# Attention score tiles of 128 queries of one head instead of 64 queries of two heads

## The chip, the cores and the metric

The kernel runs on one core of a Trainium2 chip. The metric is device time in microseconds (us) of one execution. Three runs of the kernel before took 1049.56, 1049.65 and 1050.9 us; their median is 1049.65.

## The reference

Attention with a block-causal mask feeds two dense layers. Everything is float32.

```python
B, H, S, D = 4, 8, 576, 64
scores = (1 / np.sqrt(D)) * np.matmul(q, k.transpose(0, 1, 3, 2))
mask = block_i >= block_j          # blocks of 64 positions
scores = np.where(mask, scores, -1e9)
attn = np.exp(scores - scores.max(-1, keepdims=True))
attn = attn / (attn.sum(-1, keepdims=True) + 1e-09)
x = np.matmul(attn, v)             # then to 2304 tokens x 512
h = x @ w_in                       # 512 -> 2048
x = (h - np.tanh(h)) @ w_out       # 2048 -> 512
xn = x / rms(x) * rms_g
g = xn @ w_gate; val = xn @ w_val  # 512 -> 1536 each
out = (silu(g) * val) @ w_out2     # 1536 -> 512
```

A query in block n (64 queries) sees the keys of blocks 0 to n.

## The kernel before

**Stages.** Tokens are taken in six groups of 384. Group b (0 to 3) holds queries 0 to 383 of batch b; groups 4 and 5 hold queries 384 to 575 of two batches each. A `Unit` is one batch's part of a group: part 0 (queries 0 to 383) or part 1 (384 to 575). It is worked in four head pairs p. So there are 16 head pairs of part 0 and 16 of part 1. Group 0's attention runs alone at the start, until about 49 us. After it the loop over s = 0 to 95 does the first dense layer, 16 column blocks per group (L913 to L915, L706 to L708, L716 in group 0), and `aslot` puts steps of the next groups' attention between its matmuls; attention ends near 549 us. The second dense layer with its weights follows, from about 616 us to the end.

**Light and heavy.** Units of groups 0 and 1 are light: one float32 matmul per product (two instructions in the trace). The others are heavy: a value is split into a high and a low part in fp32r, and a product is three matmuls (high by high, high by low, low by high).

**Scores (L473 to L513).** A score tile holds 64 queries of both heads of the pair: its stationary operand is a block-diagonal q (`qbd`, or `qlight` for light units; 128 rows, of which head 0 fills rows 0 to 63 of its columns and head 1 rows 64 to 127), and the moving operand is k of both heads, one above the other on the 128 rows. Tile n has exactly the keys that its queries see, 64(n+1) of them: 64, 128, 192, 256, 320, 384 in part 0, and 448, 512, 576 in part 1 (576 as two spans of 288 in two PSUM banks). So no masking is needed. VectorE takes the scaled minimum out of PSUM (L495), ScalarE the exponential with its sum (L497), GpSimd zeroes the unused half of the last block (L500), and after three tiles the reciprocal of the sums is taken (L505, L506) and the tiles are scaled, by GpSimd if light (L511), by ScalarE if heavy (L513).

**Turning (L515 to L532).** TensorE transposes each tile in 128x128 blocks (L526); ScalarE and VectorE write them to `pp`, split in high and low if heavy (L102, L107). **Value products.** `av` (L534) does one head per step; the light form `av_light` (L571, matmul in L579) uses v of one head, 64 columns, as the stationary operand and writes partitions 0 to 63 (head 0) or 64 to 127 (head 1) of one bank, six instructions a step.

**Order.** TensorE's order is the program's. `plan` (L370) writes the list of steps: three score tiles make a period, and a period's tiles are turned two periods later, with the value products (`a`) of a head pair behind its last scores. `upto` (L401) releases the steps by a cost (keys + 150 for a score tile or a turning, 400 for a value step) over the 61 slots of a group. The other engines' order is found by a planner with a timeline. PSUM has 8 banks `t` in the first stage, and 5 after it, shared by scores, turnings, value products and the first layer's `h`. `zero_q` (L211) zeroes the unused halves of the six q tiles at the start.

Of the kernel before, what the change touches and what calls it, by code (L numbers as in the profile page):

```python
# [53 lines left out]
AVLEAD = 3  # L54


class Unit:


    def __init__(self, b, part):  # L60
        self.b = b
        first, last = (0, 6) if part == 0 else (6, 9)
        self.q0, self.q1 = 64 * first, 64 * last
        self.nq = self.q1 - self.q0
        self.tiles = [(64 * (i + 1), i // 2 + 1) for i in range(first, last)]
        self.halves = [range(a, a + 3) for a in range(0, len(self.tiles), 3)]
        self.nk = self.q1
        self.nb = -(-self.nk // 128)
        self.group = b if part == 0 else B + b // 2
        self.light = self.group < 2  # L70
        self.off = 0 if part == 0 else 192 * (b % 2)

    def offset(self, ti):
        return 128 * sum(self.tiles[t][1] for t in range(ti // 3 * 3, ti))

    def blocks(self, pp, x, ti):

        c, nb = 64 * ti, self.tiles[ti][1]
        if self.q0:
            return pp[:, 0:nb * 768].rearrange("p (j h x c) -> p j h x c", j=nb, h=2, x=2)[:, :, :, x, c:c + 64]  # L80
        a, c = c // 256 * 256, c % 256
        r = pp[:, a:a + 3584].rearrange("p (h x r) -> p h x r", h=2, x=2)[:, :, x, 0:nb * 256]
        return r.rearrange("p h (j c) -> p j h c", j=nb)[:, :, :, c:c + 64]
# [10 lines left out]
def build(ctx, tc, q, k, v, w_in, w_out, w_gate, w_val, w_out2, rms_g, ident_in, out):  # L94
# [84 lines left out]
    qbd = [[at.tile([128, 6, 2, 64], F32R, name=f"q{x}{n}", bufs=1) for x in "hl"] for n in range(2)]  # L179
    lq = tc.tile_pool(name="lq", bufs=1, side="right")  # L180
    lqp = lq.__enter__()
    qlight = [lqp.tile([128, 6, 2, 64], F32, name=f"qf{n}") for n in range(2)]
# [28 lines left out]
    def zero_q():  # L211
        def none(t, hh):
            return t[64 * hh:64 * hh + 64, :, 1 - hh, :]
        for hh in range(2):
            for t in qlight:
                POOL.memset(none(t, hh), 0.0)
            for t in sum(qbd, []):
                POOL.tensor_copy(out=none(t, hh), in_=none(qlight[0], hh))

    def diag(t, hh, nq):  # L220
        return t[64 * hh:64 * hh + 64, 0:nq // 64, hh, :]

    def part(t, hh, nq):
        return t[64 * hh:64 * hh + 64, 0:nq].rearrange("p (i c) -> p i c", c=64)
# [4 lines left out]
    def reorder(name, src, eng):  # L229

        t = at.tile([128, S], F32, name=name, tag=name, bufs=1)
# [18 lines left out]
    def tr_prep(u, p, d):  # L250
# [12 lines left out]
        def q1():  # L263
            ps = tr(0)
            for hh in range(2):
                rnd(DVE if u.light and (hh == 0 or u.group or p) else ACT, diag(d["q"][0], hh, TG), part(ps, hh, TG))
            if not u.light:
                for hh in range(2):
                    lo(DVE, diag(d["q"][1], hh, TG), part(ps, hh, TG), diag(d["q"][0], hh, TG))
# [6 lines left out]
    def load_kq(src, b, p, name, r0, r1):  # L276
        t = at.tile([128, S], F32, name=name, tag=name)
# [7 lines left out]
    def kq_loads(u, p):  # L285
        d = {}
        if by_rows(u):
            for name, src in (("kr", k), ("qr", q)):
                d[name] = at.tile([128, S], F32, name=name, tag=name)
# [43 lines left out]
    def unit_prep(u, p, d):  # L333
# [14 lines left out]
        def q1():  # L348
            qt = at.tile([128, S], F32, name="qt", tag="qt", bufs=1)
            DVE.transpose(qt[:, 0:nq], qr[:, 0:nq])  # L350
            for hh in range(2):
                rnd(ACT, diag(d["q"][0], hh, nq), part(qt, hh, nq))
            for hh in range(2):
                lo(DVE, diag(d["q"][1], hh, nq), part(qt, hh, nq), diag(d["q"][0], hh, nq))

        return [(None, k1), (None, k2), (("s", 1, -1), q1), None, *values_prep(u, d)]

    class Attn:
# [11 lines left out]
        def plan(self, units):  # L370
# [5 lines left out]
            for i, (u, p) in enumerate(self.pairs):  # L376
                for half in u.halves:
                    period.setdefault(m, ([], [], []))[0].extend(("s", i, t) for t in half)
                    period.setdefault(m + 2, ([], [], []))[1].extend(("t", i, t) for t in half)
                    m += 1  # L380
                period.setdefault(m + 2, ([], [], []))[2].extend(("a", i, hh) for hh in range(2))
            for n in sorted(period):
                sc, tr, av = period[n]
                self.seq += sc[0:2] + av + tr[0:1] + sc[2:3] + tr[1:]
            self.cost = [0]
            for m, (kind, n, t) in enumerate(self.seq):
# [3 lines left out]
                self.cost.append(self.cost[-1] + (u.tiles[t][0] + 150 if kind in "st" else 400))  # L390
# [33 lines left out]
        def prep(self, cur):  # L424
            self.value(-1)
            if not self.preps and self.nextprep < len(self.pairs) and self.nextprep <= cur + 1:
# [4 lines left out]
                self.loads[i]["q"] = qlight[i % 2:i % 2 + 1] if u.light else qbd[i % 2]  # L431
# [41 lines left out]
        def scores(self, i, u, ti, d):  # L473
            keys, nb = u.tiles[ti]
            q, kh = d["q"], d["kh"]
            terms = [(q[0], kh)] if u.light else [(q[0], kh), (q[0], d["kl"]), (q[1], kh)]
            spans = [(0, keys)] if keys <= 512 else [(0, keys // 2), (keys // 2, keys)]
            sts = []
            for a, z in spans:
                s = env["t"].tile([128, 512], F32, name="t", tag="t")  # L480
                for n, (x, y) in enumerate(terms):
                    PE.matmul(s[:, 0:z - a], lhsT=x[:, ti].rearrange("p h c -> p (h c)"), rhs=y[:, a:z],  # L482
                              start=(n == 0), stop=(n == len(terms) - 1))
                sts.append((s, a, z))
            if ti == 0:
                d["st"] = at.tile([128, 24], F32, name="stat", tag="stat", bufs=3)
            if ti % 3 == 0:
                d["pt", ti // 3] = at.tile([128, 1664], F32, name="pt", tag="pt", bufs=3)
            st = d["st"]
            off = u.offset(ti)  # L490
            pt = d["pt", ti // 3][:, off:off + nb * 128]
# [807 lines left out]
```

## Time and profile before

| what | value |
|---|---|
| median of three runs | 1049.65 us |
| profiled execution | 1050.38 us |
| its span, first to last instruction | 1048.6 us |
| TensorE matmul busy | 1024.9 us |
| VectorE, ScalarE, GpSimd busy | 780.7, 664.6, 351.4 us |
| granted TensorE clock, mean | 1.000 of full |

The span is what the trace covers; 1.8 us of the profiled execution lie around it. In the timeline and in the groups PE is TensorE's matmul side and PEld its weight loading, which runs beside it. Matmuls are pipelined: the length of one is from its start to the modelled end of its results, so what one costs in a stream is read from the distance between starts.

### The profile page before, as it was taken

To read this page: it belongs to the slowest core of one execution; us is meant where nothing else is said; L and a number is where in the kernel's file an instruction comes from. 1 tells how busy PE (TensorE), PEld (TensorE's weight loads), DVE (VectorE), ACT (ScalarE), POOL (GpSimd) and SP (SyncE) were. 2 spreads that over 40 slices of the span, in tenths; PEclk is the share of its full clock that TensorE was granted. 3 is DMA by queue.
4 is the path that set the end of the run, shared out by engine and by line. 5 is a ranking of instruction groups with operands and counts; after the bars stand their busy time and mean duration, and the time that the engine had idled before them with its cause. 6 is when DMAs were issued, how large, how long until landed. Compare 5 with 4: busy or idle time off the path is not lost.

```text
span 1048.6 us, 18052 instructions
## 1 busy us (share of the span) xinstructions
PE 1024.9 (98%) x6014; PEld 934.2 (89%) x6014; DVE 780.7 (74%) x1557; ACT 664.6 (63%) x1533; POOL 351.4 (34%) x467
## 2 busy tenths in 40 slices
PE   8899999999999999999999999999999999999998
PEld 5666668998889889998999989998999999999998
DVE  5988857776787776788667889877876668666775
ACT  6977768788888877788858666443742147422253
POOL 5621111123343233334432443448211281111710
PEclk9999999999999999999999999999999999999999
DMA  9998899979777599768759979799698757876654
GB/s 217 273 291 286 269 295 268 295 207 281 208 229 208 138 256 288 216 205 289 263 167 341 358 262 347 266 352 348 228 328 300 270 197 263 309 268 247 257 220 144
DMA packets 190958, 274.03 MB, mean 261 GB/s; under 512 B 109456, under 2 KB 151184, under 8 KB 184464
## 3 DMA queue, kind: packets, MB, share of 16 engines
q1 hardware_dynamic: 190864, 272.87, 79.4%
q8 instruction: 48, 0.79, 0.3%
q14 instruction: 46, 0.38, 0.1%
HBM read 209.39 MB, written 63.44 MB: 260 GB/s over the span
## 4 chain that ended last, share of the span: by engine, by line
PE 70%; DVE 12%; DMA 7%; ACT 7%; issue 4%; POOL 0%; DVEq 0%; SPq 0%; ACTq 0%; POOLq 0%
PE t L482 5%; PE t L913 5%; PE t L915 4%; PE t L914 4%; PE acc L706 4%; PE acc L708 4%; PE acc L707 4%; PE gv L1014 4%; PE gv L1016 4%; PE gv L1015 4%; PE t L526 3%; PE ga L708 2%; PE ga L706 2%; PE ga L707 2%; PE t L550 2%
## 5 line engine op out<-in xcount | busy, mean ns | idle before, releaser
L913 PE MATMUL t<-xh,w 128*128 128x384 f32 x384 | 137.2, 357 | 0.9 <-DVE pp L107 0.8
L915 PE MATMUL t<-xh,w 128*128 128x384 f32 x384 | 129.6, 338 | 0.0
L914 PE MATMUL t<-xl,w 128*128 128x384 f32 x384 | 129.3, 337 | 0.0
L1014 PE MATMUL gv<-xh,ws 128*128 128x384 f32 x308 | 103.4, 336 | 2.3 <-DMA ws<-w2d 2.3
L1016 PE MATMUL gv<-xh,ws 128*128 128x384 f32 x308 | 103.4, 336 | 0.0
L1015 PE MATMUL gv<-xl,ws 128*128 128x384 f32 x308 | 103.4, 336 | 0.0
L706 PE MATMUL acc<-w,gh 128*128 128x512 f32 x240 | 98.7, 411 | 1.5 <-ACT gh L102 1.2
L497 ACT ACTIVATE pt<-pt,stat 128x64 f32<-128x64 f32 (+2 forms) x144 | 80.4, 559 | 23.5 <-DVE pt L495 22.7
L708 PE MATMUL acc<-w,gl 128*128 128x512 f32 x240 | 94.9, 396 | 0.3 <-DVE gl L107 0.3
L707 PE MATMUL acc<-w,gh 128*128 128x512 f32 x240 | 94.4, 393 | 0.0
L1068 ACT ACTIVATE gt<-c 128x384 f32<-128x384 f32 x29 | 15.2, 524 | 117.2 <-DVE c L1067 117.2
L1071 POOL TENSOR_TENSOR g<-va,vb 128x384 f32<-128x384 f32 x29 | 31.1, 1073 | 147.6 <-ACT va L1070 136.6
L495 DVE TENSOR_SCALAR_CACHE_REDUCE pt<-t 128x64 f32<-128x64 f32 (+2 forms) x144 | 64.0, 450 | 20.4 <-PE t L482 19.4
L913 PEld LDWEIGHTS t<-xh,w 128*128 128x128 f32 x384 | 72.3, 188 | 5.1 <-DVE pp L107 1.2
L914 PEld LDWEIGHTS t<-xl,w 128*128 128x128 f32 x384 | 72.4, 189 | 2.3
L915 PEld LDWEIGHTS t<-xh,w 128*128 128x128 f32 x384 | 72.1, 188 | 0.0
L102 ACT ACTIVATE pp<-t 128x512 fp32r<-128x512 f32 (+6 forms) x152 | 63.0, 436 | 11.1 <-PE t L526 10.7
L107 DVE TENSOR_TENSOR pp<-t,pp 128x512 fp32r<-128x512 f32 (+3 forms) x112 | 55.2, 509 | 17.2 <-ACT pp L102 16.7
L526 PE MATMUL t<-ident,pt 128*128 128x128 f32 x400 | 65.7, 273 | 2.1 <-POOL pt L511 2.1
L107 DVE TENSOR_TENSOR gl<-gt,gh 128x384 fp32r<-128x384 f32 x80 | 53.9, 674 | 16.7 <-ACT gh L102 16.4
L107 POOL TENSOR_TENSOR vp<-vr,vp 128x640 fp32r<-128x640 f32 (+1 forms) x24 | 34.1, 1421 | 93.2 <-ACT vp L102 87.3
L526 PEld LDWEIGHTS t<-ident,pt 128*128 128x128 f32 x400 | 50.5, 140 | 16.4 <-issue 5.1
(210 smaller groups left out, 3184.1 us busy)
## 6 DMA issues: line engine op xcount, KB each, us to landing
ws<-w2d SPq DMA_DIRECT2D x26, 1792.0 KB, 7.7
w<-w1d_i SPq DMA_DIRECT2D x68, 512.0 KB, 5.2
ws<-wod SPq DMA_DIRECT2D x21, 1536.0 KB, 6.6
w<-w1d_o SPq DMA_DIRECT2D x52, 512.0 KB, 5.3
st<-in_moe_w_out SPq DMA_DIRECT2D x28, 512.0 KB, 4.7
w2d<-wc SPq DMA_DIRECT2D x9, 1024.0 KB, 6.8
st<-in_moe_w_in SPq DMA_DIRECT2D x16, 512.0 KB, 5.4
w1d_i<-w SPq DMA_DIRECT2D x16, 512.0 KB, 4.8
```

The lines of the kernel that those rows point to most:

```text
L107: eng.tensor_tensor(out=o, in0=full, in1=hi.bitcast(F32), op=ALU.subtract)
L497: ACT.activation(out=pt[:, 0:keys], in_=pt[:, 0:keys], func=AF.Exp, scale=-1.0, bias=least, accum_out=st[:, 8 + ti:9 + ti])
L526: PE.transpose(t[:, (j - a) * 128:(j - a + 1) * 128], pt[:, j * 128:(j + 1) * 128], ident)
L706: PE.matmul(acc, lhsT=gh[:, c], rhs=wh, start=first, stop=False, skip_group_check=more)
L707: PE.matmul(acc, lhsT=gh[:, c], rhs=wl, start=False, stop=False, skip_group_check=more)
L708: PE.matmul(acc, lhsT=gl[:, c], rhs=wh, start=False, stop=last, skip_group_check=more)
L913: PE.matmul(h, lhsT=wh[:, c], rhs=xh[:, kk], start=(kk == 0), stop=False)
L914: PE.matmul(h, lhsT=wh[:, c], rhs=xl[:, kk], start=False, stop=False)
L915: PE.matmul(h, lhsT=wl[:, c], rhs=xh[:, kk], start=False, stop=(kk == KD - 1))
L1014: PE.matmul(ps, lhsT=wh[:, c], rhs=xh[:, kk], start=(first and kk == 0), stop=False)
L1015: PE.matmul(ps, lhsT=wh[:, c], rhs=xl[:, kk], start=False, stop=False)
L1016: PE.matmul(ps, lhsT=wl[:, c], rhs=xh[:, kk], start=False, stop=(last and kk == nk - 1))
```

## The change

A score tile of part 0 becomes 128 queries of one head. Tiles 2n and 2n+1 are head 0 and head 1 of queries 128n to 128n+127, with 128(n+1) keys: 128, 128, 256, 256, 384, 384. The stationary operand is the plain transposed q (`qsplit`, 128 columns), of which head 0 uses rows 0 to 63 and head 1 rows 64 to 127; the two heads' matmuls alternate, each into a bank of its own. The first 64 queries of a tile must not see its last 64 keys: a bf16 matmul with one row (`rowmask`: 64 ones and 64 zeros by 64 times -2^33) adds to those 64 columns. Part 1 has one such pair (512 keys) and one tile of the last 64 queries of both heads (`qlast`, block-diagonal, 576 keys as two spans of 288, as before). Periods become two tiles in part 0 (three, as before, in part 1), and turnings come `BACK` = 3 periods behind. `L500` no longer has anything to do in part 0. The light value products of both heads become one step, heads alternating, of cost 800. q is converted in one operation over 128 partitions where it took one for each head; the q tiles shrink, the `pt` buffers go from 3 to 4.

```diff
-        self.tiles = [(64 * (i + 1), i // 2 + 1) for i in range(first, last)]
-        self.halves = [range(a, a + 3) for a in range(0, len(self.tiles), 3)]
+        self.tiles = [(128 * (n + 1), n + 1) for n in ((0, 0, 1, 1, 2, 2) if part == 0 else (3, 3))]
+        self.parts = [(0, 1), (2, 3), (4, 5)] if part == 0 else [(0, 1, 2)]
+        if part:
+            self.tiles.append((S, 5))
...
     def zero_q():
...
+        POOL.memset(qlight[0], 0.0)
+        for t in qlast:
+            POOL.tensor_copy(out=t, in_=qlight[0][:, 0:128].rearrange("p (h c) -> p h c", h=2))
...
         def q1():
             ps = tr(0)
-            for hh in range(2):
-                rnd(DVE if u.light and (hh == 0 or u.group or p) else ACT, diag(d["q"][0], hh, TG), part(ps, hh, TG))
+            rnd(DVE if u.light else ACT, d["q"][0], ps)
...
-                for half in u.halves:
-                    period.setdefault(m, ([], [], []))[0].extend(("s", i, t) for t in half)
-                    period.setdefault(m + 2, ([], [], []))[1].extend(("t", i, t) for t in half)
+                for part in u.parts:
+                    period.setdefault(m, ([], [], []))[0].extend(("s", i, part[a:a + 2]) for a in range(0, len(part), 2))
+                    period.setdefault(m + BACK, ([], [], []))[1].extend(("t", i, t) for t in part)
                     m += 1
-                period.setdefault(m + 2, ([], [], []))[2].extend(("a", i, hh) for hh in range(2))
+                period.setdefault(m + BACK, ([], [], []))[2].extend(("a", i, hh) for hh in range(1 if u.light else 2))
...
-                self.seq += sc[0:2] + av + tr[0:1] + sc[2:3] + tr[1:]
+                self.seq += sc[0:1] + av + tr[0:1] + sc[1:2] + tr[1:]
...
+        def scores(self, i, u, tis, d):
+            q, kh = (qlast if u.single(tis[0]) else d["q"]), d["kh"]
+            terms = [(0, kh)] if u.light else [(0, kh), (0, d["kl"]), (1, kh)]
...
+            keys, nb = u.tiles[tis[0]]
+            c = slice(0, 128) if u.q0 else slice(128 * nb - 128, 128 * nb)
+            banks = [env["t"].tile([128, 512], F32, name="t", tag="t") for hh in range(2)]
+            for n, (x, y) in enumerate(terms):
+                for hh, s in enumerate(banks):
+                    r = slice(64 * hh, 64 * hh + 64)
+                    PE.matmul(s[:, 0:keys], lhsT=q[x][r, c], rhs=y[r, 0:keys], start=(n == 0), stop=False)
+            for hh, s in enumerate(banks):
+                r = slice(64 * hh, 64 * hh + 1)
+                PE.matmul(s[:, keys - 64:keys], lhsT=rowmask[r, 0:128], rhs=rowmask[r, 128:192], start=False, stop=True)
+            for ti, s in zip(tis, banks):
+                self.probs(i, u, ti, d, [(s, 0, keys)])
...
+        def av_light(self, u, p, d):
             nq = u.nq
+            o = env["t"].tile([128, 512], F32, name="t", tag="t")
             for j in range(u.nb):
+                for hh in range(2):
+                    src, s = u.cols(d["pp"], hh, 0, j)
+                    PE.matmul(o[64 * hh:64 * hh + 64, s:nq], lhsT=d["v"](j, hh), rhs=src.bitcast(F32),
+                              start=(j == 0), stop=(j == u.nb - 1), skip_group_check=True)
...
+        POOL.memset(rowmask[:, 0:64], 1.0)
+        POOL.memset(rowmask[:, 64:128], 0.0)
+        POOL.memset(rowmask[:, 128:192], MASKED)
         zero_q()
```

`probs` is the second half of the former `scores` (L485 to L513), unchanged but for the parts.

## Rows read from the trace of the kernel before

**Rows 1.** The page, part 1: busy us, share of span, instructions.

```profile
PE 1024.9 (98%) x6014; PEld 934.2 (89%) x6014; DVE 780.7 (74%) x1557; ACT 664.6 (63%) x1533; POOL 351.4 (34%) x467
```

**Rows 2.** Stretches: start:end, length, then PE, PEld, DVE, ACT, POOL busy.

```profile
0.00:49.00 49.00, 40.56 (x221) 28.58 (x222) 35.73 (x123) 37.94 (x121) 30.41 (x71) 1.00 0.97 246
49.00:153.00 104.00, 102.76 (x464) 71.01 (x463) 81.32 (x181) 73.81 (x183) 21.69 (x40) 1.00 0.90 290
153.00:549.00 396.00, 392.24 (x2216) 356.59 (x2215) 294.53 (x682) 316.97 (x766) 128.66 (x189) 1.00 0.79 233
```

**Rows 3.** Waits of PE, 49 to 549 us: total, times, longest (largest line first).

```profile
PE t L482 <- DVE pp L107: 1.8, 3, 1.4
...
PE t L482 <- DVE pt L495: 0.4, 1, 0.4
PE acc L706 <- DVE x2s L724: 0.2, 1, 0.2
```

**Rows 4.** Timeline of PE, heavy score tiles: start, us, instruction, count.

```profile
303.59 0.27 PE L482 MATMUL t<-kl,qh 128*128 128x192 f32 x1
303.70 0.27 PE L482 MATMUL t<-kh,ql 128*128 128x192 f32 x1
...
305.52 0.29 PE L482 MATMUL t<-kl,qh 128*128 128x256 f32 x1
305.65 0.28 PE L482 MATMUL t<-kh,ql 128*128 128x256 f32 x1
305.76 0.39 PE L706 MATMUL acc<-w,gh 128*128 128x512 f32 x1
...
463.30 0.39 PE L482 MATMUL t<-kh,qh 128*128 128x512 f32 x1
463.53 0.39 PE L482 MATMUL t<-kl,qh 128*128 128x512 f32 x1
...
470.53 0.29 PE L482 MATMUL t<-kh,qh 128*128 128x288 f32 x1
470.66 0.29 PE L482 MATMUL t<-kl,qh 128*128 128x288 f32 x1
```

**Rows 5.** Timeline of PE, light score tile and light value products.

```profile
107.59 0.81 PE L482 MATMUL t<-kh,qf 128*128 128x384 f32 x2
108.24 0.59 PE L716 MATMUL acc<-w,gh 128*128 128x512 f32 x1
...
67.92 1.02 PE L716 MATMUL acc<-w,gh 128*128 128x512 f32 x2
68.87 1.51 PE L579 MATMUL t<-pp,vp 128*64 128x384 f32 x6
70.31 1.13 PE L716 MATMUL acc<-w,gh 128*128 128x512 f32 x2
```

**Rows 6.** Timeline of PE in the first stage: value products of both heads together.

```profile
21.23 2.21 PE L579 MATMUL t<-pp,vn 128*64 128x384 f32 x12 [0.95 <-ACT pp L102]
23.38 0.33 PE L526 MATMUL t<-ident,pt 128*128 128x128 f32 x1
```

**Rows 7.** Groups by form: busy us, mean ns of one, idle before, releaser.

```profile
L107 DVE TENSOR_TENSOR ql<-qt,qh 64x192 fp32r<-64x192 f32 x32 | 18.0, 561 | 0.5
...
L497 ACT ACTIVATE pt<-pt,stat 128x384 f32<-128x384 f32 x16 | 9.8, 612 | 0.7 <-DVE pt L495 0.6
...
L505 ACT ACTIVATE stat<-stat 128x3 f32<-128x3 f32 x48 | 9.7, 202 | 0.3
...
L495 DVE TENSOR_SCALAR_CACHE_REDUCE pt<-t 128x384 f32<-128x384 f32 x16 | 8.8, 550 | 2.0 <-PE t L482 1.9
...
L104 DVE COPY qf<-t 64x384 f32<-64x384 f32 x15 | 8.3, 553 | 6.3 <-PE t L239 6.0
...
L497 ACT ACTIVATE pt<-pt,stat 128x256 f32<-128x256 f32 x16 | 8.1, 506 | 0.5 <-DVE pt L495 0.5
...
L495 DVE TENSOR_SCALAR_CACHE_REDUCE pt<-t 128x256 f32<-128x256 f32 x16 | 6.6, 412 | 1.9 <-PE t L482 1.9
```

More of the change, by code (lines that the diff above doesn't have):

```diff
@@ L73, in offset, with part, single @@
     def offset(self, ti):
-        return 128 * sum(self.tiles[t][1] for t in range(ti // 3 * 3, ti))
+        return 128 * sum(self.tiles[t][1] for t in range(self.part(ti)[0], ti))
+    def part(self, ti):
+        return next(r for r in self.parts if ti in r)
+    def single(self, ti):
+        return ti == 2 and self.q0 > 0
     def blocks(self, pp, x, ti):
-        c, nb = 64 * ti, self.tiles[ti][1]
+        nb = self.tiles[ti][1]
         if self.q0:
[L80 to L83, printed above, removed]
+            r = pp[:, 0:nb * 768].rearrange("p (j h x c) -> p j h x c", j=nb, h=2, x=2)[:, :, :, x]
+            return r[:, :, :, 128:192] if self.single(ti) else r[:, :, ti, 0:128]
+        a = 896 * (2 * (ti % 2) + x) + ti // 2 * 128
+        return pp[:, a:a + nb * 256].rearrange("p (j c) -> p j c", j=nb)[:, :, 0:128]
     def cols(self, pp, hh, x, j):
@@ L229, in reorder @@
     def reorder(name, src, eng):
-        t = at.tile([128, S], F32, name=name, tag=name, bufs=1)
+        t = at.tile([128, S if name == "kt" else 512], F32, name=name, tag=name, bufs=1)
         r = src[0:96, 0:512].rearrange("p (h t d) -> p t h d", h=2, t=4)
@@ L264, in q1 @@
             ps = tr(0)
[L265 to L266 removed]
+            rnd(DVE if u.light else ACT, d["q"][0], ps)
             if not u.light:
[L268 to L269 removed]
+                lo(DVE, d["q"][1], ps, d["q"][0])
         if u.light:
@@ L276, in load_kq @@
     def load_kq(src, b, p, name, r0, r1):
-        t = at.tile([128, S], F32, name=name, tag=name)
+        t = at.tile([128, S if name == "kr" else 512], F32, name=name, tag=name)
         for a in range(4):
@@ L348, in q1, with q2 @@
         def q1():
-            qt = at.tile([128, S], F32, name="qt", tag="qt", bufs=1)
+            qt = at.tile([128, 512], F32, name="qt", tag="qt", bufs=1)
             DVE.transpose(qt[:, 0:nq], qr[:, 0:nq])
-            for hh in range(2):
[L352 to L356, printed above, removed]
+            n = nq if nq == TG else 128
+            rnd(ACT, d["q"][0][:, 0:n], qt[:, 0:n])
+            lo(DVE, d["q"][1][:, 0:n], qt[:, 0:n], d["q"][0][:, 0:n])
+            d["qt"] = qt
+        def q2():
+            for hh in range(2):
+                r = slice(64 * hh, 64 * hh + 64)
+                rnd(ACT, qlast[0][r, hh], d["qt"][r, 128:192])
+                lo(DVE, qlast[1][r, hh], d["qt"][r, 128:192], qlast[0][r, hh])
+        more = [(("s", 2, -1), q2)] if u.q0 else []
+        return [(None, k1), (None, k2), (("s", 1, -1), q1), *more, None, *values_prep(u, d)]
     class Attn:
@@ L389, in plan @@
                     self.end[u.group] = m + 1
-                self.cost.append(self.cost[-1] + (u.tiles[t][0] + 150 if kind in "st" else 400))
+                size = 800 if u.light else 400
+                if kind != "a":
+                    size = sum(u.tiles[a][0] + 150 for a in ([t] if kind == "t" else t))
+                self.cost.append(self.cost[-1] + size)
             self.pos = 0
@@ L501, in scores @@
             self.events.add(("s", i, ti))
-            if ti % 3 < 2:
+            if ti != part[-1]:
                 return
-            r = st[:, 16 + ti - 2:17 + ti]
-            ACT.activation(out=r, in_=st[:, 8 + ti - 2:9 + ti], func=AF.Copy, bias=1e-9)
+            r = st[:, 16 + part[0]:17 + ti]
+            ACT.activation(out=r, in_=st[:, 8 + part[0]:9 + ti], func=AF.Copy, bias=1e-9)
             DVE.reciprocal(r, r)
-            for t in range(ti - 2, ti + 1):
+            for t in part:
                 o, keys_ = u.offset(t), u.tiles[t][0]
-                pv = d["pt", ti // 3][:, o:o + keys_]
+                pv = d["pt", part][:, o:o + keys_]
                 if u.light:
```

77 lines of the change are left out of this document (33 added, 44 removed).

## The prediction

> **What bounds the kernel now.** I read the page's busy times first: TensorE is at 98% of the span, VectorE at 74%, ScalarE at 63% [rows 1]. Cut into stages, the reader is to see that this holds where the change acts: from 49 to 153 us (first layer of group 0, attention of group 1) PE is busy 102.8 of 104 us, from 153 to 549 us (heavy attention beside the first layer) 392 of 396, while VectorE and ScalarE stand at 71 to 80% [rows 2]. Only the first 49 us differ: PE 40.6, ScalarE 37.9 and VectorE 35.7 of 49, taking turns. Since modelled ends can hide idle time, I read PE's waits too: from 49 to 549 us the largest of six lines is 1.8 us, and waits for the bank of a score tile (L495) come to 0.4 us [rows 3]. So up to 549 us what a step costs in PE's stream is what it costs in the end; the second layer, from 616 us, runs none of the changed steps.
>
> **What PE pays per matmul.** Distances between starts, from the timelines. Heavy: 0.11 us at 192 columns, 0.12 at 256 (0.13 and 0.11), 0.13 at 288, 0.23 at 512 [rows 4]; between them 0.145 at 320, 0.175 at 384, 0.20 at 448. Below 192 columns I take 0.11 as a floor, an estimate: the loading of the next 128 weight columns. Light: 384 columns take 0.65 us in two instructions, so 0.325 each [rows 5], and in proportion 0.27 at 320, 0.217 at 256, 0.163 at 192, 0.11 below.
>
> **What a change of array shape costs.** The only such step now is the light value product (64 weight columns). Before it stand two 512-column matmuls, 1.02 us long together; one alone is 0.59, so the step is 0.43 and their streaming ends at 68.78. The value product starts at 68.87: 0.09 us lost. It holds PE for 1.44 us until 70.31, where its own columns (twice 768 at 0.325 for 384) need 1.30: 0.14 lost. The two matmuls behind it last 1.13 instead of 1.02: 0.11 lost, a weight load that nothing hides [rows 5]. Together 1.64 us for 1.30 of streaming, 0.34 lost. For a shape with 128 weight columns I add 0.06 (a load of 0.11 instead of about half of it): 0.40 us for each excursion into half-height matmuls, an estimate.
>
> **Do halves run side by side?** No row shows two half-height matmuls. The nearest is the first stage, where both heads' value products stand next to each other on different column halves: twelve instructions in 2.15 us (21.23 to 23.38) where twice one step would be 2.88 [rows 6]. So they overlap in part although the program lists them one head after the other. I take the two row halves, listed alternately, as fully side by side (second matmul free); the other bound is that it costs its whole stream.
> The Trainium skill, "TensorE: Matmul & The Clock Gate", section "Measured speedup vs the span model", gives 3.07 times for four row tiles, not 4; in proportion each pair's stream would be 1.30 times as long, which adds 7.8 us to the sum below. No run here shows row tiles; its consequence is rival 3.
>
> **The mask matmul.** Two per pair, 64 columns each. Lower bound: 0.03 us, 64 columns at the slope between 288 and 512 columns, all else hidden. Upper bound: 0.31, if one row is a shape of its own: 0.09 to empty, 0.11 load, 0.11 floor. I take 0.10, nearer the lower, since its load can go beside the last stream.
>
> **The sum, per head pair, in PE's stream**
> - Heavy part 0, 8 head pairs. Before: 3 x (0.11 x 3 + 0.12 + 0.145 + 0.175) = 2.31 us. After: 3 x (0.11 + 0.12 + 0.175) = 1.22, and three excursions at 0.40 with masks at 0.10, 1.50: 2.72. +0.41 each, +3.2 us.
> - Part 1, 16 head pairs. Before: 3 x (0.20 + 0.23) + 6 x 0.13 = 2.07. After: 0.69 for the pair, 0.50, and 0.78 for the tile of both heads: 1.97. -1.6 us.
> - Light scores of group 1, 4 head pairs. Before: 2 x (0.11 + 0.11 + 0.163 + 0.217 + 0.27 + 0.325) = 2.39. After: 2 x (0.11 + 0.217 + 0.325) + 1.50 = 2.80. +1.6 us.
> - Light value products of group 1, 4 head pairs. Before two excursions of 1.64, after one with both heads side by side, 1.64 + 0.06 for the second head's first load: -1.58 each, -6.3 us.
> Together -3.1 us. The halves are thus nearly paid back by the excursions, and the value products carry the gain.
>
> **The other engines.** The rows of scores grow from 1344 to 1536 columns in part 0: VectorE (550 - 412)/128 = 1.08 ns a column, 0.21 us a head pair; ScalarE 0.83 ns, 0.16 us for the exponential and as much again for the heavy scaling; a third period in place of two adds one sum copy of 0.20 [rows 7]. Against it, q is converted at once: one VectorE operation of 0.55 less in a light pair, and in part 1 two of 0.56 become one and two smaller. These lie beside PE, with 20% of VectorE and ScalarE free; cost nothing. Without that cover the part-0 growth of 0.5 us over the 12 head pairs after 49 us would be 6 us. Nothing is added to SP's queue. `zero_q` loses most of its GpSimd work ahead of the first scores, which wait for q and not for it: nothing.
>
> **First stage.** ScalarE gains 4 x 0.36 us less one q conversion of 0.49, and the value products shorten from 2.15 to 1.50 us, four times, on a chain that passes through them; PE's three added excursions fall into its idle time. I take 0, between -2 and +2.
>
> **Waits.** A pair takes two of the five `t` banks at once and VectorE empties them in turn (0.55 + 0.08 us for one). PE's next pair or `h` may stand behind it. Turnings come three periods of two tiles later where they came two of three, the same six tiles in part 0, and nine instead of six in part 1, so data are no later. I take +0.5 us (bounds 0 and 52 pairs x 0.63 = 33).
>
> Sum: -3.1 + 0.5 = -2.6 us on the profiled 1050.38 (span 1048.6 and 1.8 around it), 1047.8. The median is 0.73 lower, so the forecast is **1047 us**. What the measurement can tell from no change is about 0.2%, 2.1 us; the forecast is just beyond it.
>
> **Rivals**
> 1. *Going to half height empties nothing* (the loss of rows 5 belongs to column halves alone). An excursion then costs only the masks, 0.06: part 0 -7.3, part 1 -8.6, light scores -3.6, value products -6.3, some 26 us less, 1024. VectorE and ScalarE, then at over 80%, give a little back: 1026. For it: rows stay on their own partitions. Against it: the loss in rows 5 is an emptying before and an unhidden load after, and both would be met by any reshaping. The skill's "TensorEngine Tiling (Array Packing)", section "Key Properties", says that changing the mode drains TensorE; by it this rival is out.
> 2. *Weights of the two halves load one after the other.* A step of a pair then takes at least 0.22 us: part 0 adds 3 x (0.66 - 0.405) = 0.77 x 8 = 6.1, light 0.23 x 4 = 0.9, the first load of 52 pairs 0.11 each 5.7: 12.7, 1060. For it: in rows 4 a full-height load alone sets the floor of 0.11. Against: each half reads its own partitions.
> 3. *Half-height matmuls don't run side by side, or only in part; slower.* The second streams of 8 + 16 + 4 head pairs are 1.22 x 8 + 0.69 x 16 + 1.30 x 4 = 26 us. If a share s of them is paid, s over 0.10 takes the gain away; s = 0.30 gives 1055, s = 1 gives 1073. Its place is every score pair. Against it: rows 6.
> 4. *Banks run short.* If each of 52 pairs holds PE up by 0.25 us (two fifths of a VectorE reduction), +13, 1060. Against it: 0.4 us of such waits now [rows 3].
>
> **Chances.** Forecast 0.45 (own range 1041 to 1059: masks between their bounds are -4 to +11, the first stage 2 either way), rival 1 0.22, rival 2 0.13, rival 3 0.10, rival 4 0.10. Range 1030 to 1064: it cuts off about half of rival 1 and the worse half of rival 3, with a little of the masks' end. Faster: 0.25 of the forecast's share and rival 1, 0.47. Within 0.2%: 0.13, from the forecast. Slower: 0.07 and rivals 2 to 4, 0.40.
>
> **What would show it.** Side by side: starts of a pair's two matmuls within some hundredths of a us, and three pairs of steps of 384 columns in about 0.53 us; one after the other would show double. Excursions: 0.09 us between the end of streaming and the first half-height start, and a first matmul 0.11 longer behind it. Masks: the last matmul of a pair to the next full-height start over 0.3 us means a shape of its own. Value products: one group of twelve instructions in 1.5 us in group 1. Banks: waits of PE for L495's successor over 5 us between 49 and 549. The forecast fails if the stretch from 49 to 549 us shortens by more than 10 us, or grows.

## The result, and the profile after

The changed kernel takes 1059.1 us (median of 7 runs, 1052.9 to 1062.4) where the kernel before takes 1050.4: a ratio of 1.0081, 95% interval 1.0064 to 1.0097. It is slower by 8.7 us; forecast were 1047 us. The profiled execution took 1059.36 us, span 1057.6. Medians here and below leave out three single runs of 1113 to 3563 us (one of e4, one of g1, one of the kernel before).

The page of the kernel after, answering to [rows 1], with the granted clock in 40 slices (tenths):

```profile
PE 1030.6 (97%) x6142; PEld 914.6 (86%) x6142; DVE 777.3 (73%) x1574; ACT 668.6 (63%) x1556; POOL 336.6 (32%) x397
...
PEclk9799999999999999999999999999999999999999
```

Its stretches, answering to [rows 2] (after the five busy times: granted clock, DMA share, GB/s), and three stretches inside them:

```profile
0.00:49.00 49.00, 42.45 (x245) 24.68 (x247) 34.23 (x120) 36.69 (x120) 23.11 (x47) 0.88 0.93 241
49.00:153.00 104.00, 100.25 (x492) 66.33 (x490) 80.63 (x183) 76.84 (x193) 20.69 (x30) 0.98 0.88 287
153.00:549.00 396.00, 389.75 (x2254) 337.57 (x2254) 290.09 (x694) 316.57 (x776) 120.78 (x151) 1.00 0.80 232
33.40:40.30 6.90, 6.46 (x30) 3.45 (x29) 4.59 (x17) 4.71 (x15) 2.63 (x4) 0.51 1.08 302
...
77.80:81.20 3.40, 3.40 (x10) 2.65 (x9) 2.69 (x8) 2.23 (x8) 0.00 (x0) 0.50 0.95 233
170.00:173.40 3.40, 3.40 (x10) 2.62 (x9) 3.01 (x10) 2.16 (x10) 0.00 (x0) 0.50 0.98 284
```

PE's busy time fell in both later stretches, yet the kernel is longer, and there are stretches at a clock of 0.50 (the lower level, 1.2 GHz), which the kernel before did not show up to 549 us. PE's waits from 49 to 549 us, answering to [rows 3]; the ten lines sum to 9.9 us where the six of before sum to 4.8:

```profile
PE t L501 <- DVE pp L117: 2.2, 2, 1.8
PE t L248 <- DVE pp L117: 1.4, 1, 1.4
PE t L552 <- DVE xl L117: 1.3, 1, 1.3
PE t L501 <- DVE xl L117: 1.0, 1, 1.0
...
```

The timeline of the kernel after, in order of time: value products of both heads in the first stage and of group 1 (answering to [rows 6] and [rows 5]), two waits with what follows them, and a heavy score pair of 384 columns (answering to [rows 4]). In a light pair each head's matmul is two instructions, so the line at 75.40 is the pair's first head and the one at 77.06 its second:

```profile
24.88 1.52 PE L606 MATMUL t<-pp,vn 128*64 128x384 f32 x12
...
69.48 0.33 PE L944 MATMUL t<-xh,w 128*128 128x384 f32 x1
69.74 1.52 PE L606 MATMUL t<-pp,vp 128*64 128x384 f32 x12
71.18 2.84 PE L745 MATMUL acc<-w,gh 128*128 128x512 f32 x6
...
75.40 0.70 PE L501 MATMUL t<-kh,qf 64*128 64x256 f32 x2
77.06 0.70 PE L501 MATMUL t<-kh,qf 64*128 64x256 f32 x2 [0.97 <-DVE xl L117]
77.69 0.20 PE L504 MATMUL t<-rowmask 1*128 1x64 bf16 x2
77.83 0.69 PE L942 MATMUL t<-xh,w 128*128 128x384 f32 x1
78.31 0.52 PE L943 MATMUL t<-xl,w 128*128 128x384 f32 x1
78.63 0.52 PE L944 MATMUL t<-xh,w 128*128 128x384 f32 x1
...
167.57 0.69 DVE L753 TENSOR_TENSOR x2s<-acc,g_bc 128x512 f32<-128x512 f32 x1 [1.91 <-ACT gt L950]
168.18 1.01 DVE L117 TENSOR_TENSOR pp<-t,pp 128x384 fp32r<-128x384 f32 x2
168.87 0.52 PE L248 MATMUL t<-ident,kt 96*128 96x96 f32 x4 [1.40 <-DVE pp L117]
...
201.58 0.40 PE L737 MATMUL acc<-w,gl 128*128 128x512 f32 x1
201.91 0.44 PE L501 MATMUL t<-kh,qh 64*128 64x384 f32 x2
202.19 0.34 PE L501 MATMUL t<-kl,qh 64*128 64x384 f32 x2
202.36 0.34 PE L501 MATMUL t<-kh,ql 64*128 64x384 f32 x2
202.63 0.20 PE L504 MATMUL t<-rowmask 1*128 1x64 bf16 x2
202.76 0.50 PE L735 MATMUL acc<-w,gh 128*128 128x512 f32 x1
```

The pair shows the stream as forecast: two matmuls of 384 columns (x2) start 4 ns apart (201.908 and 201.912 in the trace), are modelled 0.34 us long like a single one (L944), and the next two start 0.17 later, so the second half is free. The value products of both heads start 0.09 us after the streaming of the matmul before (69.48 + 0.17) and hold PE for 1.44. The two waits are the new thing: behind the one at 77.06 the distance of `h` matmuls is 0.32 us (78.31 to 78.63) where it is 0.17 at full clock.

**Where the time went, by stage.** S0 to S5 are the stages of the first layer of groups 0 to 5, each from the first `h` matmul of its group (L942, before L913) to that of the next, S5 to the first of the second layer. "Stream" is the sum of undisturbed start-to-start distances of its matmuls: those of the prediction, with heavy pairs at 0.82, 0.89, 1.06 and 1.22 us for 128, 256, 384 and 512 columns, light pairs at 0.71, 0.97 and 1.18 and a value step of either kind at 1.64, as undisturbed ones stand in the traces. "Rest" goes from there to the end of the span. f8, f6 and f7 are experiments below.

| us | first stage | S0 | S1 | S2 | S3 | S4 | S5 | rest |
|---|---|---|---|---|---|---|---|---|
| stream, before | | 102.6 | 89.9 | 107.2 | 89.5 | 99.3 | 73.4 | |
| stream, after | | 97.9 | 93.1 | 108.7 | 87.6 | 98.5 | 73.4 | |
| before | 48.7 | 104.7 | 90.4 | 112.3 | 91.5 | 101.0 | 76.2 | 423.8 |
| after | 51.2 | 103.5 | 96.9 | 111.3 | 89.7 | 103.0 | 77.2 | 424.8 |
| f8 (before, half loads and third buffer) | 48.3 | 103.2 | 90.4 | 112.4 | 91.5 | 101.0 | 79.1 | 421.4 |
| f6 (value products, both edits) | 47.5 | 101.0 | 90.4 | 112.5 | 91.5 | 101.0 | 80.0 | 421.6 |
| f7 (after, both edits) | 46.7 | 102.5 | 94.2 | 111.6 | 89.9 | 105.8 | 80.6 | 421.6 |

From S0 to S4 the stream fell by 2.7 us (488.5 to 485.8), the time rose by 4.5 (499.9 to 504.4). What stands over the stream went from 11.4 to 18.6 us, by 7.2; PE's waits make 5.1 of it and the two stretches at half clock at most 3.4. The other half of the span's 9.0 us lies outside: 2.5 in the first stage, 2.0 in S5 and the rest, which run nothing that was changed.

### The profile page after: what moved, and what is told of

Read it like the earlier page. It is cut to its first block, busy times and chain, and to the rows that moved or that the text cites. A ratio compares the mean times of both kernels' runs of the same rounds, so it can differ in the third digit from the quotient of the medians.

```text
span 1057.6 us, 18249 instructions
## 1 busy us (share of the span) xinstructions
PE 1030.6 (97%) x6142; PEld 914.6 (86%) x6142; DVE 777.3 (73%) x1574; ACT 668.6 (63%) x1556; POOL 336.6 (32%) x397
## 4 chain that ended last, share of the span: by engine, by line
PE 61%; DVE 9%; DMA 5%; ACT 4%; issue 3%; POOL 1%; SPq 0%; DVEq 0%; ACTq 0%; POOLq 0%
PE acc L735 4%; PE t L942 4%; PE acc L737 4%; PE acc L736 4%; PE t L944 4%; PE gv L1043 4%; PE t L943 4%; PE gv L1044 4%; PE gv L1045 4%; PE ga L737 2%; PE t L552 2%; PE ga L735 2%; PE ga L736 2%; DMA st<-in_moe_w_val 2%; PE t L501 2%
## 5 line engine op out<-in xcount | busy, mean ns | idle before, releaser
L942 PE MATMUL t<-xh,w 128*128 128x384 f32 x384 | 140.4, 366 | 0.1
L944 PE MATMUL t<-xh,w 128*128 128x384 f32 x384 | 130.0, 339 | 0.0
L735 PE MATMUL acc<-w,gh 128*128 128x512 f32 x240 | 100.6, 419 | 2.6 <-ACT gh L112 1.7
L523 ACT ACTIVATE pt<-pt,stat 128x128 f32<-128x128 f32 (+2 forms) x144 | 83.0, 578 | 27.7 <-DVE pt L521 27.1
L736 PE MATMUL acc<-w,gh 128*128 128x512 f32 x240 | 95.2, 397 | 0.0
L942 PEld LDWEIGHTS t<-xh,w 128*128 128x128 f32 x384 | 72.5, 189 | 4.3 <-issue 1.1
L521 DVE TENSOR_SCALAR_CACHE_REDUCE pt<-t 128x128 f32<-128x128 f32 (+2 forms) x144 | 64.6, 479 | 12.4 <-PE t L504 10.0
L944 PEld LDWEIGHTS t<-xh,w 128*128 128x128 f32 x384 | 72.4, 189 | 0.0
L112 ACT ACTIVATE pp<-t 128x512 fp32r<-128x512 f32 (+6 forms) x152 | 63.2, 436 | 11.4 <-PE t L552 10.8
L117 DVE TENSOR_TENSOR gl<-gt,gh 128x384 fp32r<-128x384 f32 x80 | 56.6, 707 | 17.5 <-ACT gh L112 17.2
L956 DVE TENSOR_TENSOR gt<-t,gt 128x384 f32<-128x384 f32 x80 | 44.1, 551 | 30.0 <-ACT gt L950 29.6
```

Of the source, the lines that this page charges most:

```text
L117: eng.tensor_tensor(out=o, in0=full, in1=hi.bitcast(F32), op=ALU.subtract)
L523: ACT.activation(out=pt[:, 0:keys], in_=pt[:, 0:keys], func=AF.Exp, scale=-1.0, bias=least, accum_out=st[:, 8 + ti:9 + ti])
L735: PE.matmul(acc, lhsT=gh[:, c], rhs=wh, start=first, stop=False, skip_group_check=more)
L736: PE.matmul(acc, lhsT=gh[:, c], rhs=wl, start=False, stop=False, skip_group_check=more)
L942: PE.matmul(h, lhsT=wh[:, c], rhs=xh[:, kk], start=(kk == 0), stop=False)
L944: PE.matmul(h, lhsT=wl[:, c], rhs=xh[:, kk], start=False, stop=(kk == KD - 1))
```

## The experiments

Times are medians; the ratio is to the kernel before on the same chip, with its 95% interval.

### One part at a time

**e1_values_alone**: the kernel before with only the light value products of both heads in one step.

```diff
-                period.setdefault(m + 2, ([], [], []))[2].extend(("a", i, hh) for hh in range(2))
+                period.setdefault(m + 2, ([], [], []))[2].extend(("a", i, hh) for hh in range(1 if u.light else 2))
...
-                return self.av_light(u, p, hh, d)
+                self.events.add(("a", i, 1))
+                return self.av_light(u, p, d)
```

> The kernel before with one part of the change alone: the light value products of both heads in one step, heads alternating; scores, periods and q as before. Stream theory: one excursion of 1.64 us where there were two, four times in group 1, so 6.3 us less than before, near 1044, and the first stage no longer. Clock theory (any matmul on half of the array lowers the granted clock): dips to half clock somewhere in the first 150 us and under 4 us gained, 1047 or more. Wait theory (the new order of scores and turnings makes PE wait): the order is the old one here, so as the stream theory.

1050.3, ratio 1.0002 (0.9986 to 1.0018): nothing gained. S0 lasts 103.7 us, though its stream is 96.1. The stretch of e1, then ScalarE's largest waits and PE's largest from 49 to 153 us:

```profile
49.00:153.00 104.00, 98.71 (x466) 69.66 (x467) 82.56 (x182) 74.78 (x185) 24.38 (x43) 0.98 0.89 293
```

```profile
ACT pt L497 <- DVE pt L495: 8.2, 11, 1.4
ACT cv L140 <- DMA st<-in_moe_w_in: 6.2, 3, 2.7
```

```profile
PE t L526 <- DVE xl L107: 3.0, 1, 3.0
```

PE has become idle for 5.3 us where it was for 1.2, DMA's share stays at 0.89, ScalarE stands for staged weights, and one stretch of 3.4 us is at half clock (from 143.5 us).

**e2_light_as_before**: the changed kernel with light score tiles of 64 queries as before. **e4_no_mask**: the changed kernel without the mask matmuls, so its sums run over keys that a query must not see. **e5_part1_and_values**: part 0 as before, part 1 and the value products as changed. **e9_back2**: turnings two periods behind, and so three `pt` buffers for four. The edits of e2 (its first part), e4 and e9:

```diff
+        self.old = g < 2
+        if self.old:
+            self.tiles = [(64 * (i + 1), i // 2 + 1) for i in range(first, last)]
+            self.parts = [(0, 1, 2), (3, 4, 5)]
...
-                    PE.matmul(s[:, 0:keys], lhsT=q[x][r, c], rhs=y[r, 0:keys], start=(n == 0), stop=False)
-            for hh, s in enumerate(banks):
-                r = slice(64 * hh, 64 * hh + 1)
-                PE.matmul(s[:, keys - 64:keys], lhsT=rowmask[r, 0:128], rhs=rowmask[r, 128:192], start=False, stop=True)
+                    PE.matmul(s[:, 0:keys], lhsT=q[x][r, c], rhs=y[r, 0:keys], start=(n == 0), stop=(n == len(terms) - 1))
...
-BACK = 3
+BACK = 2
```

e5 is e2's edit with `part == 0` in place of `g < 2`, so that heavy part 0 keeps its old tiles and block-diagonal q too, and with `BACK = 2`.

> The changed kernel with the score tiles of the light units (groups 0 and 1) as before: 64 queries of both heads, full height, no mask; turnings three periods of three tiles behind. Heavy units and value products as in the change. Clock theory (half-height matmuls lower the granted clock): the three dips of the changed kernel before 82 us are gone, the first stage is back from 51 to 49 us, one dip of 3.4 us at half clock less beside the first layer (1.7 us) and 1.8 us of streaming less: 1053. Wait theory (waits of PE come from the later turnings and the two banks of a pair, and the clock falls only behind such waits): little but the 1.8 us, 1056 to 1058, dips still there after waits.

> The changed kernel without its mask matmuls, so the first 64 queries of each pair's tile also see its last 64 keys; all else the same. Excursions of heavy pairs now take 0.82, 0.89, 1.06 and 1.23 us at 128, 256, 384 and 512 columns, which is 0.15 over 0.40 and three streams. If a mask is a shape of its own (0.09 to empty, then its own time), 52 pairs get 0.15 us shorter, 7.8 us in all, near 1051, with dips of the clock as before. If it is the one-row matmuls that let the clock fall, the dips go as well: 1043 to 1046. If masks were hidden, no change.

> The kernel before with the value products in one step and with the pair tile of 512 keys and the tile of both heads in part 1 alone; part 0 (light and heavy) has tiles of 64 queries as before, turnings two periods behind as before. Stream theory: 6.3 us less from the value products and 16 times 0.06 less from part 1 (1.29 before for 448 and 512 columns, 1.23 for the pair): 1043. Clock theory: half-height pairs are here only after 300 us, one in some 12 us, so at most one dip: 1043 to 1046. If the loss of the changed kernel sits in part 1 (waits for two banks there), 1048 or more.

> The changed kernel with the turnings two periods behind the scores (BACK = 2), so four tiles of 128 queries behind in part 0 instead of six, and six instead of nine in part 1, with three buffers of scaled tiles instead of four. Order theory (the later turnings put scores, turnings and the first layer's h in each other's way in the five banks): some of the loss goes, 1053 to 1056. VectorE theory: the turnings stand nearer to their scores and wait more for VectorE and ScalarE: 1059 to 1065.

| | us | ratio | (1 - mean clock) x mean time |
|---|---|---|---|
| before | 1050.4 | 1 | 1.8 |
| after | 1059.1 | 1.0081 (1.0064 to 1.0097) | 7.4 |
| e1 | 1050.3 | 1.0002 (0.9986 to 1.0018) | 5.1 |
| e2 | 1060.6 | 1.0100 (1.0078 to 1.0122) | 7.8 |
| e4 | 1056.2 | 1.0059 (1.0039 to 1.0078) | 12.3 |
| e5 | 1054.7 | 1.0034 (1.0016 to 1.0052) | 8.2 |
| e9 | 1069.2 | 1.0187 (1.0159 to 1.0214) | 15.5 |

The last column is the most that the granted clock can have cost, and can be far too much: one run of the kernel before shows a mean clock of 0.948, a bound of 54.7 us, at 1052.4 us. No part alone explains the loss. The value products take 6.3 us of stream away and gain nothing (e1). Part 1's tiles on top of them (e5) add 4.3 us, with intervals that just touch, though their stream is about 1 us shorter. Heavy part 0 with the later turnings on top of that (e2) adds 5.9, of which 3.7 are stream (8 head pairs at 2.77 for 2.31). Light scores as before cost no less than changed ones, and e2 misses both of its theories. In e5's profile, where the pairs of part 1 begin at 207 us and not after 300, the loss doesn't stand at them: S2 lasts 119.0 us for 112.3, with a wait of VectorE for a store, PE behind it, and half clock from 267.0 to 273.8:

```profile
268.55 0.69 DVE L789 TENSOR_TENSOR x2s<-acc,g_bc 128x512 f32<-128x512 f32 x1 [4.12 <-DMA x2d<-x2s]
...
269.29 0.80 PE L771 MATMUL acc<-w,gh 128*128 128x512 f32 x1 [4.32 <-DVE x2s L789]
```

Without masks a heavy pair of 384 columns holds PE for 0.72 us (200.41 to 201.13) where it was 0.85 (201.91 to 202.76), so a pair's masks cost 0.13:

```profile
200.41 0.44 PE L501 MATMUL t<-kh,qh 64*128 64x384 f32 x2
...
200.87 0.34 PE L501 MATMUL t<-kh,ql 64*128 64x384 f32 x2
201.13 0.50 PE L732 MATMUL acc<-w,gh 128*128 128x512 f32 x1
```

So the kernel should lose 6.8 us of stream (52 pairs) and loses 2.9, with intervals that overlap, while the clock's bound rises by 4.9: what the stream gains, idle time and clock take back, as far as can be told. Turning a period earlier costs 10 us more, so three periods in place of two are no loss in the changed kernel.

### VectorE's load

**e6, e7, e8**: before, after, and e1, each without the clamp in `convert`, one 128x512 VectorE operation for each staged block. It changes only weights near the end of float32's range; the reference's inputs have none.

```diff
-        pin(DVE.tensor_scalar(f, f, HIGHEST * REBIAS, 0.0, ALU.min, ALU.max))
```

> The kernel before without the clamp in its weight conversion (L143, 68 VectorE operations of 0.52 us, 32 of them ahead of 153 us): a base for the next two runs, in which VectorE has some 17 us less to do in the first 153 us. It changes the values only of weights near the end of float32's range, of which there are none. PE is busy 98.8% of 49 to 153 us in the kernel before, so little comes of it: 1047 to 1050.

> The changed kernel without the same clamp. VectorE theory (what PE saves turns into waits for VectorE's queue, whose order is full of conversions, and the clock falls behind those waits): with 17 us of VectorE's work gone before 153 us most of the loss goes, within 3 us of the light-convert base. Clock theory (half-array matmuls lower the clock by themselves): the difference to the base stays 7 to 10 us and the mean clock stays near 0.993. Order theory (the later turnings and the pairs' two banks make PE wait): the same 7 to 10 us.

> The kernel before with the value products of both heads in one step alone, without the clamp. VectorE theory: the 6 us of PE's stream that this saves in group 1, and that came to nothing with the clamp, come out: 5 to 6 us under the light-convert base. Clock theory (column halves lower the clock): under 3 us.

e6 1043.4, 0.9934 (0.9913 to 0.9954); e7 1051.6, 1.0010 (0.9992 to 1.0028); e8 1044.2, 0.9940 (0.9920 to 0.9959). Every kernel gets 6 to 7.5 us faster, more than was expected of e6, and the distance of after to before stays at 8.2. This part of VectorE's load prices all of them alike and is not what the change met. Leaving the clamp out is a saving of its own. How the rest of VectorE's work is ordered was not tried.

### Staged loads

**f3, f4, f5**: before, e1, and after, fetching half of every staged block. The conversion, left out below, reads that half twice, so that its operations keep their sizes and half of the weights are wrong.

```diff
-        SP.dma_start(out=o, in_=src)
+        if len(src.shape) == 3:
+            SP.dma_start(out=o[:, 0:2], in_=src[:, 0:2])
+        else:
+            SP.dma_start(out=o[:, 0:512], in_=src[:, 0:512])
...
```

> The kernel before with only the first half of every staged weight block fetched (256 KB in place of 512 KB); the conversion reads that half twice, so all instructions of ACT, DVE and POOL keep their sizes, and the products use wrong weights for the other half. DMA theory (the stretch 49 to 153 us is set by the staged loads, DMA share 0.9 to 1.0 there): the first stage and the first attention stage get shorter by several us, the total falls by 4 to 10 us under 1050.4. Rival (the stretch is set by TensorE's stream and by ACT's order of work, the loads only happen to fill it): within 1.5 us of 1050.4.

> The light value products of both heads in one step (as in e1), with the same half loads as f3. DMA theory: the 4 to 6 us that e1 should have gained and did not now appear, f4 is 4 to 6 us under f3, and the time ACT waits for staged weights in 49 to 153 us goes from 7.2 us to under 2. Rival (clock and ACT's order take the gain): f4 equals f3 within 1.5 us and the stretch keeps its length.

> The changed kernel with the same half loads as f3. DMA theory: the stretch 49 to 153 us shrinks by 4 to 6 us more than in f3, so the ratio to f3 is 0.998 to 1.004 (f5 minus f3 between -2 and +4 us). Rival: f5 stays 8 to 9 us over f3, as the changed kernel is over the one before.

f3 1050.8, 1.0003 (0.9990 to 1.0016); f4 1050.6, 1.0002 (0.9987 to 1.0017); f5 1056.3, 1.0058 (1.0038 to 1.0078). The DMA theory as I had put it falls: the kernel before does not get faster, nor do the value products alone. The edit has a price of its own, though: in the six profiles with half loads S5, where weights are still converted, lasts 79.1 to 80.6 us for 76.2 to 77.2, while S0 of the kernel before is 1.5 us shorter (f8). So f3's time is a sum of both, and f4 is to be compared with f3. There f4's profile shows S0 shortened (100.5 us, f3 103.1) and the gain lost at once in S1 (94.7 for 90.4). The timeline of f4 there:

```profile
156.90 0.32 SPq L727 DMA_DIRECT2D x2d<-x2s  x1
...
161.30 0.69 DVE L726 TENSOR_TENSOR x2s<-acc,g_bc 128x512 f32<-128x512 f32 x1 [3.76 <-DMA x2d<-x2s]
161.91 0.55 DVE L107 TENSOR_TENSOR pp<-t,pp 128x384 fp32r<-128x384 f32 x1
...
162.51 0.33 PE L486 MATMUL t<-kh,qh 128*128 128x128 f32 x1 [2.48 <-DVE pp L107]
...
163.34 0.77 PE L708 MATMUL acc<-w,gh 128*128 128x512 f32 x1
```

The result of a group leaves in three tiles `x2s` through two buffers. The third waits on VectorE until the store of the first has landed; behind it in VectorE's order stands an emptying of `pp`, behind that PE, and the clock falls (0.50 from 163.1 us; a 512-column product modelled at 0.77 us). VectorE's time at `x2s` for a store, 49 to 549 us: before 0, e1 1.4, f4 3.8, e5 7.2, e4 7.0, e2 8.9, e9 9.1; after 1.0, with 1.9 more at the same instruction put down to ScalarE (167.57 above).

### A third buffer

**g1, g2, g3**: before, e1, after, the third tile in a buffer of its own. **g4**: e8 with it. The edit reaches group 0's results alone, since from group 2 on another line of the kernel, which it leaves, says where `x2s` lies.

```diff
-    env["x2s"] = lambda g, t: wk.tile([128, DM], F32, name="x2s", tag="x2s")
+    env["x2s"] = lambda g, t: (lqp if t == 2 else wk).tile([128, DM], F32, name="x2s", tag="x2s")
```

> The kernel before with a buffer of its own for the third x2s tile of a group (one line). VectorE does not wait for the stores of x2s in the kernel before (0 us in 49 to 549 us), so the store theory expects no change: 1049 to 1051.5 us. The rival (order of work) expects no change either.

> The light value products of both heads in one step (e1) with the third x2s buffer. Store theory: VectorE's wait at x2s for a store (1.4 us in e1, 3.8 with half loads) goes to 0, the dip behind it too, and 2 to 4 us of the 6.3 appear: 1046 to 1048.5. Rival: as e1, 1050.3 +- 1.5.

> The changed kernel with the third x2s buffer. Store theory: the wait of 1.4 us before the turning at 169 us and the dip 170 to 173 go, waits at later group ends too; 4 to 7 us less than the changed kernel, 1052 to 1055. If the whole loss hung on it: 1047 to 1050. Rival (order of turnings and scores): 1057.5 to 1060, as the changed kernel.

> Value products of both heads, no clamp in the conversion (e8) and the third x2s buffer; the candidate for the fastest. e8's profile has no wait of VectorE for a store, so the store theory expects 0 to 1.5 us less than e8's 1044.2, the rival 0.

g1 1048.6, 0.9990 (0.9974 to 1.0005); g2 1050.4, 1.0004 (0.9990 to 1.0018); g3 1057.4, 1.0070 (1.0043 to 1.0098); g4 1041.4, 0.9913 (0.9891 to 0.9935). The buffer alone gives the value products nothing and the changed kernel 1.7 us by the medians, within the intervals. In g3's profile S1 falls from 96.9 to 94.2 us and the wait of 1.91 at 167.57 is 0.77 (at 167.97), so most of it was the store's; S0 grew by 2.2, and at the later groups' ends VectorE stands 2.6 us for stores. In g2, S0 is as long as ever (104.2): ScalarE is late there. Timeline of g2:

```profile
138.29 1.15 ACT L102 ACTIVATE w<-st 128x512 fp32r<-128x512 f32 x2
...
139.35 0.47 ACT L102 ACTIVATE pp<-t 128x384 f32<-128x384 f32 x1
...
139.96 0.52 PE L246 MATMUL t<-ident,qt 96*128 96x96 f32 x4 [1.29 <-ACT pp L102]
```

Weights stand ahead of the emptying in ScalarE's order. g4 is the fastest version tried; against e8 and e6 its gain of 2 to 3 us is within the intervals. The clock's bound is 9.5 us in g2 and 1.5 in the kernel before beside it, so the clock is a rival there for what the buffer may have given.

### Both limits off

**f6, f7, f8**: e1, after, and before, each with half loads and the third buffer; f8 is the control.

> Value products of both heads, half of each staged weight block fetched (as f4, so the products of the other half use wrong weights) and the third x2s buffer. Two limits in a row: the first attention stage as short as in f4 (100.5 us) and the second one at 90.4 in place of 94.7, so 1045.5 to 1047.5 against f3's 1050.8. ACT's order holds it: 1049.5 to 1051, as f4 and g2.

> The changed kernel with both (half loads as f5, wrong weights for the other half, and the third x2s buffer). Two limits in a row: f5's 1056.3 less the 1.7 that the buffer gave the changed kernel, and up to 3 more: 1051.5 to 1054.6. ACT's order and the new turnings: 1055 to 1057.

> The kernel before with half of each staged weight block fetched (wrong weights for the other half, as f3) and the third x2s buffer: the control for f6. If f6's gain is that of the value products: a ratio of 0.9985 to 1.0015, 1048.5 to 1051.5 us. If the two edits alone make it: 0.996 to 0.998, as f6.

f6 1046.5, 0.9969 (0.9957 to 0.9981); f8 1049.6, 0.9998 (0.9987 to 1.0009); f7 1054.5, 1.0054 (1.0035 to 1.0073). The value products now gain 3.1 us (1049.6 to 1046.5), with intervals apart, where either edit alone showed nothing. Stretches of f8, then of f6 with PE's largest wait in it:

```profile
49.00:153.00 104.00, 104.00 (x475) 72.52 (x474) 81.53 (x184) 74.92 (x188) 20.89 (x40) 1.00 0.70 228
```

```profile
49.00:153.00 104.00, 100.40 (x489) 72.25 (x489) 81.90 (x186) 77.42 (x196) 21.40 (x41) 1.00 0.71 229
```

```profile
PE t L250 <- ACT pp L102: 3.0, 2, 1.9
```

DMA's share is down to 0.7 and in f8 PE is never idle; in f6 it still is for 3.6 us. So two limits stood in a row behind PE, the staged loads in S0 and the store at group 0's end in S1. Most of what f6 still waits in S0 is for ScalarE, whose order may keep the other half of the 6.3; no run changed that order. The clock's bound is lower as well (6.0 us in f4, 9.5 in g2, 4.0 in f6), so part of the gain can be the clock's. For the changed kernel the two edits show little: f7 is 5.0 us over the kernel before on its chip, f5 was 6.0, the changed kernel 8.7, and their intervals overlap. VectorE still stands 2.1 us for stores at the later groups' ends. f7 stays 8.0 over f6.

## Why the prediction was wrong

**The step that failed** is the conclusion drawn from [rows 1 to 3]: "up to 549 us what a step costs in PE's stream is what it costs in the end". For work that is taken away it has to be asked what is late next, and the only answer given was waits for banks. From 49 to 153 us PE was nearly saturated, but DMA's share stood at 0.90 in the very row that I quoted [rows 2], and ScalarE and VectorE carry weights and emptyings in one order. They were put at nothing because 20% of each was free; that share doesn't tell what stands ahead of an emptying. Of the -6.3 us of the value products, which carried the forecast, e1 got 0 and f6, with two limits eased, 3.1. That explains why the gain didn't come; why the kernel got slower is shown only in part, as follows.

**Waits**, taken at +0.5 us, came to +5.1 in PE's waits (4.8 to 9.9). The sign set for rival 4, waits for L495's successor (L521), reads 0.7 us and not over 5. But its mechanism is there: a pair takes two of the five `t` banks at once, and the step before can still hold one with a turning or a value product that VectorE has yet to empty (`pp`, `xl`, `xs`). In four of the 52 pairs the first head had its bank and the second stood for one (0.97 us at 77.06, 0.79 at 306.13, 0.36 at 474.12, 1.82 at 491.57): 3.9 of the 9.9 us, where rival 4 had 13. Ahead of three of these four emptyings VectorE was on a weight conversion (at 75.86, 304.66 and 489.50 us); ahead of the wait at 168.87 it stood at `x2s`. No run gave the changed kernel more banks, so how much of its loss hangs on them is open.

**The clock** was not in the sum at all. Its bound rose from 1.8 to 7.4 us over all runs; in the profile two stretches of 3.4 us at half clock between 49 and 549 us cost 1.7 each at most, and one at 726 us, in unchanged work, as much. Those two stand behind waits of PE (77.06, 168.87), and heavy half-height pairs ran at full clock from 174 to 549 us. Half-height pairs are not needed for a fall. g1 has none, and its clock falls behind the same wait at the same step after which it stayed up in the kernel before:

```profile
260.59 0.33 PE L482 MATMUL t<-kh,qh 128*128 128x128 f32 x1 [1.39 <-DVE pp L107]
```

```profile
262.70:266.10 3.40, 3.40 (x12) 3.31 (x11) 1.51 (x6) 3.04 (x8) 0.00 (x0) 0.50 0.91 206
```

The first line is g1's timeline, the second its stretch behind it; in the kernel before the wait was 1.37 us (at 263.03) and the clock from 264 to 268 us 1.00. In the 20 traces the clock falls 33 times between 52 and 800 us, each time during or shortly behind one of 99 waits of PE of 0.95 us or more; 65 of these had no fall. So waits go ahead of falls, and which of them brings one is open; no run changed a wait alone.

**The stream was right.** Side by side: yes, with nothing lost (rivals 2 and 3 fall). The Trainium skill, "TensorE: Matmul & The Clock Gate", section "Measured speedup vs the span model", gives 3.07 times for four row tiles; the 1.30 taken from it in proportion doesn't hold for two, which show no loss. Excursions cost as estimated, 0.53 us with the mask for 384 columns, and rival 1 falls. The Trainium skill, "TensorEngine Tiling (Array Packing)", section "Key Properties", says that a change of tiling mode drains TensorE, and the 0.09 us at 69.74 agree. Masks cost 0.13 us and not 0.10. The emptying ahead of them (0.27 from the last pair's start to L504 where 0.17 is stream) isn't theirs: without masks the next full-height matmul starts as late (e4, 200.87 to 201.13). Sum for S0 to S4: -2.7, forecast -3.1. By parts, S0 -4.7 (1.6 - 6.3 forecast), S1 to S4 +2.0 (+1.6 forecast).

**The first stage**, taken at 0 within 2, came to +2.5 in the profile, with two stretches at half clock; f7's is 1.6 shorter than f8's. I take it for scatter; nothing tested it.

**Left open.** f7 is 8.0 us over f6, while its stream in S0 to S4 is 3.8 us longer (S0 +1.8, from 96.1 in f6). Most of the rest is in S4 (+4.8 for a stream of -0.8). There PE waits 2.6 us for `pp` from VectorE, at the second head of a pair again. f7's waits of PE, 0 to 630 us, and its timeline there:

```profile
PE t L505 <- DVE pp L117: 2.9, 2, 2.6
```

```profile
481.60 1.09 DVE L158 SCALAR_TENSOR_TENSOR cv<-cv,cu 128x512 int32<-128x512 int32 x1
482.08 0.49 PE L505 MATMUL t<-kh,qh 64*128 64x512 f32 x1
482.72 1.77 DVE L159 SCALAR_TENSOR_TENSOR fu<-st,cv 128x512 int32<-128x512 int32 x1
484.41 0.68 DVE L117 TENSOR_TENSOR pp<-t,pp 128x512 fp32r<-128x512 f32 x1
485.14 0.50 PE L505 MATMUL t<-kh,qh 64*128 64x512 f32 x1 [2.57 <-DVE pp L117]
```

Two steps of a weight conversion stand ahead of the emptying in VectorE's order, and from 486.7 us the clock is 0.50 for 3.4 us. Whether that order or the smaller q operations of part 1 make the wait was not tried.

## What to carry to other kernels

A saving on the engine that is busy 98% can be worth nothing (e1: 6.3 us of stream, no time): read the DMA share and what is queued ahead of each emptying before counting it. Banks are shared: a step that takes two at once waits for whatever else holds one, and not for its own kind alone. When removing one suspect changes nothing, remove two together, with the control: here either alone gave 1.000 and both gave 0.997. Look whether an edit reaches all the places it is meant for, and what it costs elsewhere. Half-height matmuls of two heads ran side by side at no loss here, but each excursion costs some 0.5 us with its mask (1.06 for a pair with 3 x 0.175 of stream), so it pays only where the stream saved is longer.

## What the runs showed of the hardware

A one-row matmul is a shape of its own: 0.10 us of emptying ahead of it, as ahead of a full-height one, and 0.13 until the next full-height start. Two 64-row matmuls on different halves start 4 ns apart and cost the stream of one. Halving 512 KB loads took DMA's share from 0.90 to 0.70 between 49 and 153 us and S0 of the kernel before from 104.7 to 103.2 us (f8): a share of 0.90 cost little while PE's stream filled the stretch.
